# A state-attention and soft-MoE kernel: smaller matmul tiles for the folded routing weights and for the output, and combine weights turned by one VectorE transpose

## The chip, the cores and the metric

The kernel runs on one core of one Trainium2 chip. The metric is the device time of one execution, in microseconds (us); lower is better. Five engines work side by side, each through its own instructions in order: TensorE (PE in the rows; its weight loads are listed as PEld), VectorE (DVE), ScalarE (ACT), GpSimd (POOL) and SyncE (SP), whose queue here issues every DMA.

## The reference, cut to what matters

```python
# attention: x (8,8,512,64), state (8,8,32,64)
a     = softmax(0.125 * x @ state.T)            # over the 32 states
xread = a @ state
a2    = softmax(0.125 * state @ x.T)            # over the 512 tokens
sread = a2 @ x
x = concat([xread, sread], tokens)              # 4352 tokens of 512 values
# feed-forward
g = silu(x @ w_in)                              # w_in (512, 2048), given in fp64
x = g @ w_out                                   # w_out (2048, 512), given in fp64
# soft MoE, 8 experts of 4 slots: 32 slots
logits     = x @ phi                            # phi (512, 32)
d          = softmax(logits, over all tokens)
slot_input = d.T @ x                            # (32, 512)
slot_out   = per expert: relu(slot_input @ w1[e]) @ w2[e]
c          = softmax(logits, over the 32 slots)
out        = c @ slot_out                       # (4352, 512)
```

## The kernel before, in words

All operations are first recorded by a helper class, then put in an order by a list scheduler with fixed costs of its own, and issued in that order, so each engine's order of work is fixed when the program is built. Because every operation is recorded by one helper, nearly all rows of the profile carry line 333; they are told apart by the names of their tiles. A `together` block makes one unit of several TensorE calls. A tile with a tag takes its place in a ring of buffers of that tag; PSUM has the rings `h` (2 banks), `lg` (1), `w` (1) and `w2` (4), and tiles of a ring are handed out in the order in which the program names them.

**Start.** The fp64 weights are loaded as pairs of 32-bit words, half of a quarter at a time (8 pieces `raw` of w_out, then 8 of w_in), and turned into fp32 by `conv`: one ScalarE operation and five VectorE operations on 128x1024 elements. `wo_half` (line 481) does this for w_out, writes the result `win` to a DRAM scratch (`wo_f`), turns it with TensorE transposes (`wT`), and after each second half multiplies it by phi: `w2ps` holds w_out @ phi for a quarter of the 2048 hidden units, and VectorE copies it to `w2p` (lines 505 to 513). The w_out-phi product folds the second matrix of the feed-forward and phi into one 2048x32 matrix, so that logits come straight from g. Between these steps stands the attention of the first batch (`a_scores`, `a_split`, `a_soft1` to `a_soft3`, `a_eT`, `a_sread`, whose result `srs` VectorE scales out of the PSUM tile `sr`) and the first part of the second's. `win_half` then converts w_in.

**Middle.** For each of 9 blocks of tokens (`k`; 512 tokens, the last 256) `hid` makes the hidden units (`h`, 16 pieces), ScalarE and VectorE make `g` of them, VectorE transposes `g` by 32x32 blocks into `blk`, `logits` multiplies by `w2p`, `s_sum` and `s_rep` add up the partial sums (`lr`) and make the exponentials (`dT` for the slots, `cw` for the tokens), and `s_dTg` multiplies `dT` by `blk` into the four banks `S`, which are added into `acc`.

**End.** `slot_T` turns `acc` and `slot_mm` multiplies it by w_out: once for the first 8 blocks (`siaT`, `sia`), once for the last (`sibT`, `sib`); then the experts' first matrices (`f`, to `hs`, transposed as `hT`), the combine weights (lines 1060 to 1079: each block of `cw` is split by VectorE and GpSimd into two fp32r parts, turned by TensorE as `cTp` and copied by ScalarE to `cT`), and, for each half `ch` of the 512 output columns, the experts' second matrices (`so`, `sor`) and the output matmuls `o`, evicted by VectorE and ScalarE in turn and written by SP. w1 and w2 (32 pieces of 1 MB, `in_w_dram`) are loaded by `load_w` into places that other tiles have left; pieces 17 to 20 go where `wo`, the operand of `sib`, has stood.

Of the kernel before, what the change touches and what calls it, by code (L numbers as in the profile page):

```python
# [7 lines left out]
F32 = mybir.dt.float32  # L8
F32R = mybir.dt.float32r
# [357 lines left out]
def tile_state_attention_soft_moe(  # L367
# [113 lines left out]
    def wo_half(fq, half):  # L481
        n = 2 * fq + half
        if half == 0:

            wn_t[fq] = win_t[fq]
            wT_t[fq] = unit(("wb", "wb", "A", "A")[fq], [4, 4, 4, 32], f"wT{fq}")
        wn = wn_t[fq][:, 2 * half:2 * half + 2]
        conv(n, wn)
        if n >= 4:
            next_raw()  # L490
        nc.sync.dma_start(out=wo_f32[fq, :, 2 * half:2 * half + 2], in_=wn)
        for x in range(2):
            q = 2 * half + x
            p = bank("h", f"wT{fq}_{q}")
            with nc.together():
                for dc in range(4):
                    nc.tensor.transpose(p[:, dc * 128:dc * 128 + 128], wn[:, x, dc * 128:dc * 128 + 128], ident)
            nc.scalar.copy(
                out=wT_t[fq][:, :, :, q, :], in_=p.rearrange("p (d i c) -> p d i c", d=4, i=4)
            )  # L500
        if half == 0:
            return

        wT = wT_t[fq]
        p = bank("w", f"w2ps{fq}")
        with nc.together():
            for i in range(4):
                for dc in range(4):
                    mm(
                        p[:, 32 * i:32 * i + 32], lhsT=wT[:, dc, i].rearrange("p q c -> p (q c)"),  # L510
                        rhs=phi_sb[:, dc, :], start=(dc == 0), stop=(dc == 3),
                    )
        nc.vector.tensor_copy(out=w2p[:, fq].rearrange("p i s -> p (i s)"), in_=p[:, 0:128])

    def win_half(fq, half):
        n = 8 + 2 * fq + half
# [65 lines left out]
    def a_soft3(b):  # L582
        s = at[b, "s"]
        t = s[:, 1].rearrange("p h t -> p (h t)")
        nc.vector.transpose(out=t, in_=s[:, 0].rearrange("p h t -> p (h t)"))
        at[b, "ar"] = a = unit("A", [2, 2, 512], f"ar{b}", F32R)
        nc.scalar.copy(out=a[:, 0], in_=s[:, 1])
        nc.gpsimd.tensor_tensor(out=a[:, 1], in0=s[:, 1], in1=a[:, 0].bitcast(F32), op=ALU.subtract)

    def a_eT(b, h2):  # L590
        e = at[b, "e"]
# [158 lines left out]
        nc.scalar.copy(out=ls[:, :n], in_=lg_t.pop(k)[:, :n])  # L750
        sx[k, "ls"] = ls

    def tok_major(src, nt, tag, name):

        t = rot.tile([128, 4, NSLOT], F32, tag=tag, name=name, bufs=2 if tag == "ld" else 1)
        for x in range(4):
            rows = slice(32 * x, 32 * x + 32)
            nc.vector.transpose(
                out=t[rows, :nt, :],
                in_=src[rows, :nt * 128].rearrange("p (y x r) -> p x y r", x=4, r=32)[:, x],  # L760
            )
        return t[:, :nt, :]

    def s_rep(k):
# [1 line left out]
        nt = n // 128  # L766
        ls = sx.pop((k, "ls"))
        lr = bank("w", f"lr{k}")
        mm(lr[:, :n], lhsT=r44, rhs=ls[:, :n], start=True, stop=True)
        m = rot.tile([128, 4], F32, tag="m", name=f"m{k}")  # L770
        nc.vector.reduce_max(out=m[:, 0:1], in_=lr[:, :n], axis=AX.X)
        prev = m_old[0]
# [12 lines left out]
        m_old[0] = m  # L785
        sx[k, "m"], sx[k, "first"] = m, first
        if k in BY_PE:
            dT = tok_major(d, nt, "ld", f"dT{k}")
        else:
            dT = rot.tile([128, 512], F32, tag="ld", name=f"dT{k}")  # L790
            nc.vector.transpose(out=dT[:, :n], in_=d[:, :n])
# [86 lines left out]

    def slot_T(x, name):

        p = bank("w", f"{name}T")
        with nc.together():
            for q in range(4):
                for f in range(4):
                    n = 32 * (4 * q + f)
                    mm(p[:, n:n + 32], lhsT=x[:, q, f * 128:(f + 1) * 128], rhs=r4, start=True, stop=True)
        xT = rot.tile([128, 16, NSLOT], F32, tag="g", name=f"{name}Ts", bufs=NG)
        nc.vector.tensor_copy(out=xT.rearrange("p i s -> p (i s)"), in_=p)
        return xT

    def slot_mm(xT, name):
        p = bank("w", name)
        with nc.together():
            for q in range(4):
                for fq in range(4):
                    mm(
                        p[32 * fq:32 * fq + 32, :],
                        lhsT=xT[:, 4 * q + fq, :],
                        rhs=wo_t[fq][:, q, :],
                        start=(q == 0),  # L900
                        stop=(q == 3),
                    )
        return p


# [128 lines left out]
    for w in range(2):  # L1034
        hp = [bank("h", f"f1_{w}_{x}") for x in range(2)] if w == 0 else pair("f1_1")
        for dc in range(4):
            for x in range(2):
                with nc.together():
                    for e in range(4):
# [4 lines left out]
                            start=(dc == 0),  # L1044
                            stop=(dc == 3),
                        )
        load_w(28 if w == 0 else 32)
        for x in range(2):
            hs = rot.tile([128, 512], F32, tag="th", name=f"hs{w}_{x}")
            nc.scalar.activation(out=hs, in_=hp[x], func=AF.Relu, scale=masks[:, w:w + 1])  # L1050
# [6 lines left out]
            nc.vector.tensor_copy(out=hTs[:, w, x].rearrange("p i s -> p (i s)"), in_=p)  # L1057


    cT = []  # L1060
    for q in range(NB + 1):
        nt = ntok(q) // 128
        if q == NB:
            ctu = rot.tile([128, 1, 512], F32R, tag="g", name="cT8", bufs=NG)
        elif q % 4 == 0:
            ctu = unit("wb", [4, 512], f"cT{q}", F32R)
        cv = cw[:, 4 * q:4 * q + nt, :].rearrange("p t (o s) -> p t o s", o=1).to_broadcast([128, nt, 2, NSLOT])
        c2 = rot.tile([128, 4, 2, 2, NSLOT], F32, tag="th", name=f"c2_{q}")
        hi = c2[:, :nt, :, 0, :]
        nc.vector.tensor_copy(out=hi.bitcast(F32R), in_=cv)  # L1070
        nc.gpsimd.tensor_tensor(out=c2[:, :nt, :, 1, :], in0=cv, in1=hi, op=ALU.subtract)
        p = bank("w", f"cTp{q}")
        with nc.together():
            for t in range(nt):
                nc.tensor.transpose(
                    p[:, t * 128:(t + 1) * 128], c2[:, t].rearrange("p a b s -> p (a b s)"), ident
                )
        nc.scalar.copy(out=ctu[:, q % 4, :nt * 128], in_=p[:, :nt * 128])
        cT.append(ctu[:, q % 4, :])


    outb = out.rearrange("(b r) f -> b r f", r=TOK)
    n_out = 0
    obuf = [12, 14, 16, 17, 18, 19, 20, 0, 1, 2]
    for ch in range(2):
        so = bank(("lg", "h")[ch], f"so{ch}")
        with nc.together():
            for w in range(2):
                for kk in range(8):
                    for e in range(4):  # L1090
                        mm(
                            so[32 * e:32 * e + 32, 0:256],
                            lhsT=hTs[:, w, kk // 4, kk % 4, 32 * e:32 * e + 32],
                            rhs=wt["w2", 8 * ch + 4 * w + e][kk // 2][:, 256 * (kk % 2):256 * (kk % 2) + 256],
                            start=(w == 0 and kk == 0),
                            stop=(w == 1 and kk == 7),
                        )
        sos = rot.tile([128, 256], F32, tag="ld", name=f"sos{ch}")
        nc.scalar.copy(out=sos, in_=so[:, 0:256])
        p = bank(("lg", "h")[ch], f"sor{ch}")  # L1100
        mm(p[:, 0:256], lhsT=r44, rhs=sos, start=True, stop=True)
        sor = rot.tile([128, 256], F32R, tag="th", name=f"sor{ch}")
        nc.scalar.copy(out=sor, in_=p[:, 0:256])
        nc.vector.tensor_tensor(
            out=sor[64:128, :], in0=p[64:128, 0:256], in1=sor[64:128, :].bitcast(F32), op=ALU.subtract
        )
        cols = slice(256 * ch, 256 * ch + 256)
        for q in range(NB + 1):
            nt = ntok(q) // 128
            if q % 2 == 0:  # L1110
                obu = place(obuf[5 * ch + q // 2]).rearrange("p (a t f) -> p a t f", a=2, t=4)
            ob = obu[:, q % 2]
            for t in range(0, nt, 2):
                tag = ("w", "w2", "w2", "h", "w2", "w2", "h")[n_out % 7]
                p = bank(tag, f"o{n_out}")
                with nc.together():
                    for x in range(2):
                        mm(
                            p[:, 256 * x:256 * x + 256], lhsT=cT[q][:, (t + x) * 128:(t + x + 1) * 128], rhs=sor,
                            start=True, stop=True,  # L1120
                        )
                (nc.scalar.copy if n_out % 2 else nc.vector.tensor_copy)(
                    out=ob[:, t:t + 2, :].rearrange("p t f -> p (t f)"), in_=p
                )
                n_out += 1
            if q < NB:
                nc.sync.dma_start(
                    out=outb[q, 0:512, cols].rearrange("(t p) f -> p t f", p=128), in_=ob
                )
            else:  # L1130
                for t in range(nt):
                    nc.sync.dma_start(out=outb[4 * t:4 * t + 4, 512:TOK, cols], in_=ob[:, t, :])
    for k in range(NB + 1):

        for op in exps.get(k + 1, []):
# [50 lines left out]
```

## Time and profile before

| | us |
|---|---|
| median of 3 runs (lowest, highest) | 582.49 (582.3, 584.6) |
| profiled execution | 581.93 |
| its span, first to last instruction | 580.1 |
| TensorE busy | 485.5 |
| VectorE busy | 355.6 |
| ScalarE busy | 274.6 |
| GpSimd busy | 102.9 |

The profiled execution takes 1.83 us more than its span. Shares of busy time are averages over stages that differ; the stage has to be read before a share means anything. The clock of TensorE is given as a share of full speed (1.00 is 2.4 GHz, 0.50 is 1.2 GHz).

### The profile page before, as it was taken

The numbers are of one execution on the slowest core, as the hardware profiler recorded it, in microseconds if no ns is written. First come the engines' busy times: TensorE is split into PE (matmuls) and PEld (weight loads), VectorE is DVE, ScalarE is ACT, GpSimd is POOL, SyncE is SP. The second block draws the span as 40 slices with busy tenths as digits, with TensorE's granted clock in tenths as the row PEclk, the third lists the DMA queues.
The fourth block names the chain that finished last, engine by engine and source line by source line (L and its number), as shares of the span: only waits on it lengthen the run. The fifth ranks groups of instructions, "written<-read, shape, count | busy, mean of one in ns | idle before, by whom it ended". The sixth has DMA issues, their size and how long they took to land.

```text
span 580.1 us, 10381 instructions
## 1 busy us (share of the span) xinstructions
PE 485.5 (84%) x4380; PEld 299.6 (52%) x4380; DVE 355.6 (61%) x610; ACT 274.6 (47%) x471; POOL 102.9 (18%) x65
## 2 busy tenths in 40 slices
PE   2456672897999989989989999999999997897760
PEld 1446671564646546546555555465557792434640
DVE  5776568997396676686785785784763934111430
ACT  3522331864764754754845845745735523011430
POOL 0000010001213232232232222223006330003100
PEclk9985555898999999999999999999999998799795
DMA  8975554420202202202202202103033299599796
GB/s 340 410 271 181 188 182 141 150 73 0 73 2 73 74 1 73 73 3 73 72 2 74 73 2 79 68 1 147 1 138 154 95 424 363 218 424 421 283 295 199
DMA packets 21566, 85.79 MB, mean 148 GB/s; under 512 B 1552, under 2 KB 10640, under 8 KB 13840
## 3 DMA queue, kind: packets, MB, share of 16 engines
q1 hardware_dynamic: 21520, 85.14, 39.5%
q8 instruction: 34, 0.56, 0.4%
q14 instruction: 12, 0.10, 0.0%
HBM read 72.03 MB, written 13.11 MB: 147 GB/s over the span
## 4 chain that ended last, share of the span: by engine, by line
PE 69%; DVE 17%; ACT 7%; issue 3%; POOL 1%; DMA 1%; DVEq 0%; ACTq 0%; POOLq 0%
PE h L333 31%; PE S L333 7%; DVE win L333 5%; PE w2ps L333 5%; PE wbp L333 5%; PE lg L333 4%; DVE acc L333 3%; PE f L333 2%; PE so L333 2%; PE sr L333 2%; PE wT L333 1%; ACT e L333 1%; ACT wb L333 1%; DVE lt L333 1%; DVE wb L333 1%
## 5 line engine op out<-in xcount | busy, mean ns | idle before, releaser
L333 PE MATMUL h<-ar,wb 128*128 128x512 f32 x768 | 198.9, 407 | 3.8 <-DVE wb L333 2.1
L333 PEld LDWEIGHTS h<-ar,wb 128*128 128x128 f32 x768 | 140.2, 190 | 66.1 <-issue 13.9
L333 ACT ACTIVATE g<-h 128x512 f32<-128x512 f32 (+1 forms) x108 | 62.0, 575 | 109.3 <-PE h L333 107.5
L333 DVE STREAM_TRANSPOSE blk<-g 128x512 f32<-128x512 f32 (+1 forms) x128 | 83.5, 666 | 38.2 <-ACT g L333 37.8
L333 POOL TENSOR_TENSOR wb<-wf,wb 128x512 fp32r<-128x512 f32 x28 | 36.0, 1286 | 126.3 <-ACT wf L333 81.5
L333 POOL TENSOR_TENSOR ar<-s,ar 128x1024 fp32r<-128x1024 f32 x8 | 19.1, 2388 | 179.8 <-ACT ar L333 179.8
L333 PE MATMUL wbp<-win,ss 64*32 64x512 f32 x512 | 36.4, 626 | 13.0 <-DVE win L333 13.0
L333 ACT CAST wb<-wbp 128x512 fp32r<-128x512 f32 x64 | 34.6, 595 | 26.7 <-PE wbp L333 26.7
L333 PE MATMUL lg<-g,w2p 128*32 128x512 f32 (+1 forms) x288 | 43.8, 581 | 0.0
L333 PE MATMUL S<-blk,dT 32*32 32x512 f32 (+1 forms) x992 | 38.9, 611 | 3.4 <-DVE dT L333 2.8
L333 DVE TENSOR_TENSOR wb<-wbp,wb 128x512 fp32r<-128x512 f32 x36 | 24.4, 687 | 23.6 <-ACT wb L333 23.4
L333 PE MATMUL wT<-cst,win 128*128 128x128 f32 x64 | 15.6, 424 | 24.0 <-DVE win L333 15.9
L333 POOL TENSOR_TENSOR s<-s,tm 128x1024 f32<-128x1024 f32 x12 | 23.3, 1938 | 52.3 <-DVE tm L333 37.1
L333 ACT ACTIVATE th<-h 128x512 f32<-128x512 f32 (+1 forms) x36 | 20.6, 571 | 21.9 <-PE h L333 21.9
L333 PE MATMUL w2ps<-phi,wT 128*128 128x32 f32 x128 | 28.1, 402 | 2.7 <-ACT wT L333 2.7
L333 PEld LDWEIGHTS w2ps<-phi,wT 128*128 128x128 f32 x128 | 27.6, 332 | 4.3 <-ACT wT L333 4.3
L333 PEld LDWEIGHTS wT<-cst,win 128*128 128x128 f32 x64 | 12.7, 226 | 28.8 <-issue 17.1
L333 ACT ACT_TABLE_LOAD x21 | 26.9, 1283 | 1.1 <-PEq L1176 0.7
L333 DVE TENSOR_REDUCE tm<-s 128x32 f32<-128x1024 f32 x16 | 19.4, 1214 | 13.1 <-ACT s L333 13.1
L333 ACT COPY wT<-wT 128x512 f32<-128x512 f32 x16 | 9.4, 586 | 37.6 <-PE wT L333 37.6
L333 DVE SCALAR_TENSOR_TENSOR acc<-acc,m,S 128x512 f32<-128x512 f32 x28 | 19.1, 741 | 12.2 <-PE S L333 12.2
L333 DVE SCALAR_TENSOR_TENSOR g<-th,h 128x512 f32<-128x512 f32 (+1 forms) x36 | 23.0, 646 | 4.2 <-ACT th L333 4.0
(118 smaller groups left out, 688.1 us busy)
## 6 DMA issues: line engine op xcount, KB each, us to landing
place<-in_w_dram SPq DMA_DIRECT2D x17, 1024.0 KB, 12.1
blk<-in_w_dram SPq DMA_DIRECT2D x15, 1024.0 KB, 9.4
raw<-in_w_out_dram SPq DMA_DIRECT2D x8, 1024.0 KB, 14.4
xT<-in_xT_dram SPq DMA_DIRECT2D x8, 1024.0 KB, 4.7
xk<-in_xk_dram SPq DMA_DIRECT2D x8, 1024.0 KB, 5.5
raw<-in_w_in_dram SPq DMA_DIRECT2D x8, 1024.0 KB, 4.8
out_dram<-place SPq DMA_DIRECT2D x10, 512.0 KB, 6.5
wo_f<-win SPq DMA_DIRECT2D x8, 512.0 KB, 5.8
```

The source lines that it names most:

```text
L333: made = [call(*args, **kwargs) for call, args, kwargs in op.calls]
```

## The change

Seven edits, and nothing else in the program:

1. `w2ps`: instead of 16 calls with a 128x128 piece of `wT` as weights and 32 columns of phi moving, 4 calls with phi as 128x32 weights and 512 columns of `wT` moving, in the four column tiles of one bank; ScalarE copies the bank (`w2s`, `s2`), 4 calls add up the four parts and turn them (`w2q`), and ScalarE, no longer VectorE, makes the copy to `w2p`.
2. The subtraction that makes `ar` of the first batch moves from GpSimd to VectorE.
3. `tok_major` orders the tokens of `lt` by x, y, r where it was y, x, r; `dT` of block 0 keeps the old order.
4. `slot_T` takes its bank from `w2`, `slot_mm` from `h`, where both took `w`; `sia` is made to come after `lr` of the last block.
5. Some of the calls of `load_w` stand earlier, inside the loop over `f`.
6. The combine weights: the loop over 9 blocks is replaced by one VectorE transpose of `cw` by 32x32 blocks.
7. The output: `so` is issued as 16 groups of 4 calls, not one of 64; `sor` is one fp32 copy by VectorE; `o` is made by fp32 32x32 tiles with 256 columns, two blocks of tokens into four banks at a time, and the DMAs of the two blocks follow when the four banks are copied. The last block has 4 output DMAs per half instead of 2.

```diff
-            for i in range(4):
-                for dc in range(4):
-                    mm(
-                        p[:, 32 * i:32 * i + 32], lhsT=wT[:, dc, i].rearrange("p q c -> p (q c)"),
-                        rhs=phi_sb[:, dc, :], start=(dc == 0), stop=(dc == 3),
-                    )
-        nc.vector.tensor_copy(out=w2p[:, fq].rearrange("p i s -> p (i s)"), in_=p[:, 0:128])
+            for dc in range(4):
+                mm(
+                    p[32 * dc:32 * dc + 32, :], lhsT=phi_sb[:, dc, :],
+                    rhs=wT[:, dc].rearrange("p i q c -> p (i q c)"), start=True, stop=True,
+                )
+        s2 = rot.tile([128, 512], F32, tag="ld", name=f"w2s{fq}")
+        nc.scalar.copy(out=s2, in_=p)
+        p = bank("w", f"w2q{fq}")
+        with nc.together():
+            for i in range(4):
+                mm(p[:, 32 * i:32 * i + 32], lhsT=s2[:, i * 128:(i + 1) * 128], rhs=r4, start=True, stop=True)
+        nc.scalar.copy(out=w2p[:, fq].rearrange("p i s -> p (i s)"), in_=p[:, 0:128])
...
-        nc.gpsimd.tensor_tensor(out=a[:, 1], in0=s[:, 1], in1=a[:, 0].bitcast(F32), op=ALU.subtract)
+        (nc.gpsimd if b else nc.vector).tensor_tensor(out=a[:, 1], in0=s[:, 1], in1=a[:, 0].bitcast(F32), op=ALU.subtract)
...
-        p = bank("w", f"{name}T")
+        p = bank("w2", f"{name}T")
...
-        p = bank("w", name)
+        p = bank("h", name)
...
+        if name == "sia":
+            nc.after(first, sx[NB, "lr"])
...
+            if dc == 1:
+                load_w(25 if w == 0 else 31)
+            if dc == 3:
+                load_w(28 if w == 0 else 32)
...
+    cT = unit("wb", [2048], "cT")[:, 0:34 * NSLOT]
+    nc.vector.transpose(out=cT, in_=cw.rearrange("p t s -> p (t s)"))
...
-        so = bank(("lg", "h")[ch], f"so{ch}")
-        with nc.together():
-            for w in range(2):
-                for kk in range(8):
+        so = bank("lg", f"so{ch}")
+        for w in range(2):
+            for kk in range(8):
+                with nc.together():
...
+            tags = ("w2", "w2", "w2", "w2") if q // 2 % 2 == 0 else ("h", "h", "w", "lg")
+            p = [bank(t, f"o{ch}_{q}_{x}") for x, t in enumerate(tags)]
...
+                for a in both:
+                    for y in range(nt):
+                        for x in range(4):
+                            n = NSLOT * (4 * (q + a) + y)
+                            mm(
+                                p[x][32 * y:32 * y + 32, 256 * a:256 * a + 256],
+                                lhsT=cT[32 * x:32 * x + 32, n:n + 32],
+                                rhs=sor[32 * x:32 * x + 32, :],
+                                start=True,
+                                stop=True,
+                            )
```

## Rows read from the trace of the kernel before

**Rows 1.** Waits of VectorE, first 140 us: total us, times, longest.

```profile
DVE w2p L333 <- PE w2ps L333: 19.1, 4, 6.0
DVE win L333 <- ACT win L333: 6.8, 1, 6.8
DVE srs L333 <- PE sr L333: 3.9, 1, 3.9
```

**Rows 2.** Timeline of the start: start, us, engine, operation [idle before <- releaser].

```profile
66.44 0.29 DVE L333 COPY w2p<-w2ps 128x128 f32<-128x128 f32 x1 [5.98 <-PE w2ps L333]
66.65 1.21 DVE L333 TENSOR_TENSOR win<-win,acc 128x1024 f32<-128x1024 f32 x1
...
71.75 1.22 DVE L333 TENSOR_TENSOR win<-win,acc 128x1024 f32<-128x1024 f32 x1
...
75.09 0.59 ACT L333 COPY wT<-wT 128x512 f32<-128x512 f32 x1 [0.27 <-PE wT L333]
...
75.73 7.04 PE L333 MATMUL w2ps<-phi,wT 128*128 128x32 f32 x32 [0.68 <-ACT wT L333]
...
76.72 3.42 DVE L333 SCALAR_TENSOR_TENSOR acc<-raw,acc 128x1024 f32<-128x1024 uint32 x1
...
82.80 0.29 DVE L333 COPY w2p<-w2ps 128x128 f32<-128x128 f32 x1 [2.66 <-PE w2ps L333]
...
83.15 1.11 PE L333 MATMUL eT<-cst,e 128*128 128x128 f32 x4 [0.39 <-DVE w2p L333]
...
88.73 0.48 DVE L333 TENSOR_SCALAR srs<-sr,asm 128x64 f32<-128x64 f32 x2 [3.91 <-PE sr L333]
```

**Rows 3.** Timeline: one 16-record group early and late, and a logits group.

```profile
98.87 1.96 PE L333 MATMUL wbp<-win,ss 64*32 64x512 f32 x16 [9.06 <-DVE win L333]
...
111.15 1.09 PE L333 MATMUL wbp<-win,ss 64*32 64x512 f32 x16 [1.17 <-DVE win L333]
...
112.76 1.06 PE L333 MATMUL lg<-g,w2p 128*32 128x512 f32 x8
```

**Rows 4.** Chain that ended last, whole span (start, us, what): the middle.

```profile
211.48 1.07 PE S L333 x32
...
253.94 1.07 PE S L333 x32
```

**Rows 5.** The same chain from 476 us on.

```profile
481.35 0.71 PE lr L333 x2
...
484.03 1.95 PE S L333 x32
485.98 4.41 PE sia L333 x32
...
516.55 4.43 PE f L333 x40
...
531.70 0.60 PE cTp L333 x4
...
542.87 5.12 PE o L333 x30
...
548.66 7.16 PE so L333 x128
```

**Rows 6.** Windows: stretch, us, engines busy, granted clock, DMA share, GB/s.

```profile
540.00:543.00 3.00, 1.88 (x7) 1.15 (x7) 0.43 (x1) 1.17 (x4) 0.45 (x1) 0.50 0.69 287
543.00:546.00 3.00, 3.00 (x15) 3.00 (x16) 1.83 (x3) 1.59 (x4) 0.00 (x0) 0.55 0.08 28
555.00:560.00 5.00, 3.53 (x35) 2.56 (x28) 1.71 (x4) 2.26 (x6) 0.00 (x0) 1.00 0.78 236
...
575.00:580.00 5.00, 0.00 (x0) 0.00 (x0) 0.00 (x0) 0.00 (x0) 0.00 (x0) 0.50 0.27 84
```

**Rows 7.** Window during the loads: TensorE busy, granted clock, DMA share, GB/s.

```profile
510.00:515.00 5.00, 5.00 (x52) 1.00 1.01 423
```

**Rows 8.** Group: copies out of PSUM at the output; busy us, mean ns.

```profile
L333 DVE COPY place<-o 128x512 f32<-128x512 f32 x11 | 7.0, 683 | 2.2 <-PE o L333 2.2
```

More of the change, by code (lines that the diff above doesn't have):

```diff
@@ L751, in s_sum, with tok_major @@
         sx[k, "ls"] = ls
-    def tok_major(src, nt, tag, name):
+    def tok_major(src, nt, tag, name, order="x y r"):
         t = rot.tile([128, 4, NSLOT], F32, tag=tag, name=name, bufs=2 if tag == "ld" else 1)
@@ L759, in tok_major @@
                 out=t[rows, :nt, :],
-                in_=src[rows, :nt * 128].rearrange("p (y x r) -> p x y r", x=4, r=32)[:, x],
+                in_=src[rows, :nt * 128].rearrange(f"p ({order}) -> p x y r", x=4, r=32)[:, x],
             )
@@ L768, in s_rep @@
         lr = bank("w", f"lr{k}")
-        mm(lr[:, :n], lhsT=r44, rhs=ls[:, :n], start=True, stop=True)
+        sx[k, "lr"] = mm(lr[:, :n], lhsT=r44, rhs=ls[:, :n], start=True, stop=True)
         m = rot.tile([128, 4], F32, tag="m", name=f"m{k}")
@@ L891, in slot_mm @@
     def slot_mm(xT, name):
-        p = bank("w", name)
+        p = bank("h", name)
+        first = None
         with nc.together():
@@ L895, in slot_mm @@
                 for fq in range(4):
[L896 removed]
+                    op = mm(
                         p[32 * fq:32 * fq + 32, :],
@@ L902, in slot_mm @@
                     )
+                    first = first or op
+        if name == "sia":
+            nc.after(first, sx[NB, "lr"])
         return p
@@ L1057, in tile_state_attention_soft_moe @@
             nc.vector.tensor_copy(out=hTs[:, w, x].rearrange("p i s -> p (i s)"), in_=p)
[L1060 to L1072, printed above, removed]
-        with nc.together():
[L1074 to L1079, printed above, removed]
+    cT = unit("wb", [2048], "cT")[:, 0:34 * NSLOT]
+    nc.vector.transpose(out=cT, in_=cw.rearrange("p t s -> p (t s)"))
     outb = out.rearrange("(b r) f -> b r f", r=TOK)
-    n_out = 0
     obuf = [12, 14, 16, 17, 18, 19, 20, 0, 1, 2]
     for ch in range(2):
-        so = bank(("lg", "h")[ch], f"so{ch}")
-        with nc.together():
-            for w in range(2):
-                for kk in range(8):
+        so = bank("lg", f"so{ch}")
+        for w in range(2):
+            for kk in range(8):
+                with nc.together():
                     for e in range(4):
@@ L1099, in tile_state_attention_soft_moe @@
         nc.scalar.copy(out=sos, in_=so[:, 0:256])
-        p = bank(("lg", "h")[ch], f"sor{ch}")
+        p = bank("lg", f"sor{ch}")
         mm(p[:, 0:256], lhsT=r44, rhs=sos, start=True, stop=True)
[L1102 to L1106, printed above, removed]
+        sor = rot.tile([128, 256], F32, tag="th", name=f"sor{ch}")
@@ L1107, in tile_state_attention_soft_moe @@
+        nc.vector.tensor_copy(out=sor, in_=p[:, 0:256])
         cols = slice(256 * ch, 256 * ch + 256)
-        for q in range(NB + 1):
+        for q in range(0, NB + 1, 2):
+            ob = place(obuf[5 * ch + q // 2]).rearrange("p (x a f) -> p x a f", x=4, a=2)
+            tags = ("w2", "w2", "w2", "w2") if q // 2 % 2 == 0 else ("h", "h", "w", "lg")
+            p = [bank(t, f"o{ch}_{q}_{x}") for x, t in enumerate(tags)]
             nt = ntok(q) // 128
[L1110 to L1123, printed above, removed]
@@ new lines, in tile_state_attention_soft_moe @@
+            both = range(2) if q < NB else range(1)
+            with nc.together():
+                for a in both:
[9 more added lines that the diff above has]
+                            )
@@ L1124, in tile_state_attention_soft_moe @@
+            for x in range(4):
+                r = slice(0, 32 * nt)
+                (nc.scalar.copy if x % 2 else nc.vector.tensor_copy)(
+                    out=ob[r, x, 0:len(both)].rearrange("p a f -> p (a f)"), in_=p[x][r, 0:256 * len(both)]
                 )
-                n_out += 1
             if q < NB:
-                nc.sync.dma_start(
-                    out=outb[q, 0:512, cols].rearrange("(t p) f -> p t f", p=128), in_=ob
-                )
-            else:
-                for t in range(nt):
-                    nc.sync.dma_start(out=outb[4 * t:4 * t + 4, 512:TOK, cols], in_=ob[:, t, :])
+                for a in both:
+                    nc.sync.dma_start(
+                        out=outb[q + a, 0:512, cols].rearrange("(t p) f -> p t f", p=128), in_=ob[:, :, a]
+                    )
+            else:
+                for x in range(4):
+                    nc.sync.dma_start(out=outb[2 * x:2 * x + 2, 512:TOK, cols], in_=ob[0:64, x, 0])
```

3 lines of the change are left out of this document (1 added, 2 removed).

## Prediction

> **What bounds the kernel now.** I read the waits of each engine first, then the timeline of the first 140 us, then the chain of work that ended last, and at the end the windows with the DMA share. Three stages with three limits come out.
>
> In the start the limit is VectorE. In its first 140 us it waits for four things only, and three of them stand in [rows 1]: 6.8 us for the first converted word, 19.1 us in four copies of `w2p`, each standing behind `w2ps` on TensorE, and 3.9 us before `srs`. What the reader is to see in [rows 2] is that the copy, a 0.29 us instruction, sits in front of the conversions on an in-order engine: VectorE stood 5.98 us before the copy at 66.44 us, and the conversion's last addition follows it 0.21 us later.
>
> In the middle the limit is TensorE. The chain of waits is matmul after matmul, and the `S` group comes back at 211.48 and 253.94 us, 42.46 us apart [rows 4]. No edit touches a matmul of that period, so I carry it over unchanged: what the start saves arrives at the end in full.
>
> In the end it is first TensorE, then DMA. While the experts' matrices are loaded the DMA share is 1.01 at 423 GB/s [rows 7]. Then it falls to 0.69 and to 0.08 between 540 and 546 us, and to 0.78 between 555 and 560 [rows 6]: the loads are through, and the first output isn't ready, because the transposes `cTp` run from 531.70 up to the first `o` at 542.87 [rows 5]. In 575 to 580 us the share is 0.27: the last writes drain.
>
> **The change part by part.**
>
> *Edit 1, the first three quarters.* The long waits of three copies go with the copies themselves, which ScalarE now makes. All four waits sum to 19.1 us and the fourth is 2.66 [rows 1, 2], so three are 16.4; three copies' steps of 0.21 add 0.6. Sum 17.1 us. What VectorE does next (the addition, then the next piece) needs only words that ScalarE has prepared: after the first, VectorE never waited for `win` from ScalarE [rows 1].
>
> *Edit 1, the last quarter.* Here VectorE next stands before `srs`, which hangs on TensorE: `w2ps`, `eT`, `sr`. Old path from the start of `w2ps` to the start of `eT`: 83.15 - 75.73 = 7.42 us [rows 2]. New path: 8 records of 512 columns in column tiles, which `lg` makes in 1.06 us [rows 3]. That is at the later speed; in the start the 16 records of `wbp` took 1.96 us, later 1.09 [rows 3], so 1.06 x 1.8 = 1.9. Then a copy of 128x512 out of PSUM, 0.59 [rows 2]; 8 records of the old kind, 7.04 / 32 = 0.22 each, 1.76; a copy of 128x128, 0.3 (VectorE's took 0.29); four hand-overs of about 0.07. Sum 4.8, gain 2.6 us. Bounds: nothing (should the two extra hand-overs be slow), and the whole of what VectorE loses in this piece besides, if it finds other work to do ahead of `srs`: 2.6 + 3.9, and 1.0 for edit 2 (next), 7.5. I take 2.6, because the order of instructions around `srs` comes from the same list scheduler and the wait of 3.91 stands there already.
>
> *Edit 2.* VectorE's operation at 76.72 takes 3.42 us where its neighbours of the same kind (the rows' 1.21 us addition is the nearest) take little over a third: GpSimd's subtraction runs beside it. The change takes away some 2.2 and puts one two-input operation of 1.2 on VectorE, 1.0 net. It lies inside the wait for `srs`, so I cost it at nothing; if that cover is gone it is worth the 1.0 counted in the bound above.
>
> *Edit 3* keeps number and shape of the transposes; the nearest row for a price is none better than themselves: 0. If reading the tokens in a row were slower or faster by half, it would be hidden under TensorE in every block but the last.
>
> *Edit 4.* Now TensorE ends `lr` at 482.06, stands until 484.03, makes the first half of `S`, then `sia`, then the second half [rows 5]. With a bank of its own `sia` fills the gap: 1.97 us. After the gap the first `S` half takes 1.95 us for 32 records where 1.07 is the usual [rows 4, 5], and `sia` 4.41 for 32 where 40 of `f` took 4.43, so 3.54 at that pace. Without a gap these 0.88 and 0.87 should go too. Sum 3.7 us; bounds 2.0 (the gap alone) and 3.7. I take 3.7: nothing else idles TensorE there. Loads 17 to 20 wait for the end of `sib`, so the stream of loads starts as much earlier.
>
> *Edit 5.* A load can start only when the `f` group before it has freed its place, whatever line it stands on, and at 510 us the DMA engines are already full [rows 7]. Cost 0, no gain either.
>
> *Edit 6* removes all of `cTp` and what ScalarE and VectorE do for it. The new transpose is one VectorE operation of 1088 columns, at most twice the 0.683 of a 512-column copy [rows 8], while TensorE makes `f`. From 531.70 to 542.87 are 11.2 us, of which making `sor` (one matmul like `lr`, 0.71, and two copies of 256 columns) needs about 2. TensorE could thus start `o` some 9 us earlier. But DMA then is the limit: what can be gained is the time in which it stands: 0.31 x 3 + 0.92 x 3 + 0.22 x 5 = 4.8 us [rows 6]. I take 4.8; bounds 0, and 4.8 plus the drain, 0.73 x 5 = 3.65.
>
> *Edit 7.* The output matmuls: 136 calls of 32x32 tiles per half, 272 records. 32 records of 512 columns take 1.07 us when 16 tiles work together [rows 4]; for 256 columns between half and all of that, so 4.5 to 9.1 us per half, against 5.8 from the first `o` to `so` now (542.87 to 548.66 [rows 5]). Four banks are copied by two engines, two 0.683 copies each, so the first output DMA of a half comes about 1.1 + 1.4 = 2.5 us after its first `o`. Is it hidden? Half 0: `so` ends at 531.7 - 3.7 = 528.0, `o` starts at about 530, the DMAs are queued from 532.5. The loads end near 542 - 3.7 = 538. The writes of half 0, 4.46 MB at 236 / 0.78 = 303 GB/s, then take until 552.7. Half 1 needs the last load, half of `so` (3.6 us), `sor` (2) and 2.5: 546. So there are over 6 us of cover, which also pay for four more DMAs and for the later issue of pairs of blocks. If the cover is gone, each us late is a us lost.
>
> The Trainium skill (TensorEngine Tiling, Key Properties) says that a change of tiling mode drains TensorE. Edit 7 lets groups of `so` (128x32) stand between groups of `o` (32x32), so this speaks against it. The nearest row is `lg`, which stands among 128x128 work and takes 1.06 where 8 records at the pace of `f` take 0.89: some 0.17 a change, and ten changes, two for each of five output groups, are 1.7 us, inside the cover. By the rule with nothing overlapped it would be more, which no row here prices.
>
> **Sum.** Start 17.1 + 2.6 = 19.7. End 3.7 + 4.8 = 8.5. Span 580.1 - 28.2 = 551.9; plus the 1.83 us around the span, 553.7. The median of the runs shown lies 0.56 above the profiled execution: 554.
>
> **Rivals.**
>
> *The end gives only edit 4 (0.15).* The output stage is late by its cover: banks shared by `so` and `o`, changes of tile size, pairs of blocks before a DMA. For it: one bank `lg` serves both halves of `so` and an output bank. Against: 6 us. Time 554 + 4.8 = 559; if even edit 4 is lost, 562.
>
> *The wait moves from TensorE to ScalarE (0.12).* ScalarE is in order too. If its preparing operation for the next but one piece stands behind the new copies, VectorE waits. From the end of a second half's conversion (71.75 + 1.22) to the start of `w2ps` are 2.8 us [rows 2], to the new `w2p` copy 4.8 more, and about 1.2 to prepare 1024 columns (two copies of 512 at 0.59), against 5.1 for the piece between (66.65 to 71.75): 3.7 us in each of three quarters, 11.1. Time 565. Against: no such wait now [rows 1].
>
> *More than that (0.06).* VectorE also loses the wait for `srs`, and the drain shortens: 554 - 4.9 - 3.65 = 545.5.
>
> *Slower: tiles of one column group take turns (0.04).* In `S` successive calls go along column tiles, in the new `o` along row tiles, which no row shows. One record of 512 columns alone takes 0.44 (four in 0.44 in `f`), of 256 0.22; one at a time, 272 are 60 us a half, 120 in all, where now about 17 + 6 are spent: 554 + 97 - 4.8 is over 640. It decides when a half takes more than about 23 us, that is with fewer than 2.6 tiles at work together. Against: 16 work together in `S` [rows 4].
>
> *No change (0.03).* The start's waits reappear in full elsewhere: a DMA-bound start. Against: after the first piece no row of [rows 1] names a DMA.
>
> **Chances and range.** The forecast has 0.60. Its own range takes the bounds: start 17.1 to 24.6, end 2.0 to 12.2: 545.7 to 563.4. The range over the cases, with the ScalarE rival in and the slow one out, is 544 to 566. A difference under 0.5% can't be told from none: faster 0.93, same 0.03, slower 0.04.
>
> **What would show it.** Right: no wait of VectorE for `w2ps`, and `srs` near 69 us, not 88.73; a wait for `srs` of 3 to 5 us; the period of `S` still 42.5; `lr`, `sia`, `S` without a gap, `sia` at 3.5; DMA full from the loads to the last writes. Wrong: VectorE waiting for `win` from ScalarE in the start; a longer period in the middle, since the scheduler orders the whole program anew; `o` slower than 9 us a half; DMA idle between loads and writes.

## The result and the profile after

| kernel | median of its runs, us | range | runs |
|---|---|---|---|
| before, on the same chip | 582.86 | 582.3 to 584.6 | 4 |
| after | 557.49 | 554.34 to 560.75 | 4 |

The ratio is 0.956, with an interval of 0.950 to 0.962: 25.4 us less, where 28.2 were forecast. The profiled execution took 560.75 us (span 559.0), the longest of its four. A later run of the same kernel (called the repeat below) has a span of 555.7; why one kernel has two spans comes with the clock, further down.

First the waits of VectorE in the first 122 us of the kernel after (engine, what waited <- what it waited for: us in total, times, longest):

```profile
DVE win L333 <- ACT win L333: 6.7, 1, 6.7
DVE srs L333 <- PE sr L333: 2.6, 1, 2.6
DVE ar L333 <- ACT ar L333: 1.6, 1, 1.6
...
DVE asm L333 <- ACT e L333: 0.6, 1, 0.6
```

The line of 19.1 us for `w2p` in [rows 1] is gone. The single wait for the first word is still there and no second one has joined it. The wait for `srs` is shorter than the old 3.9. Two small waits are new: the subtraction that edit 2 put on VectorE stands 1.6 us behind ScalarE's part of it, and a sum (`asm`) stands 0.6 us behind ScalarE's exponentials.

The timeline of the start of the kernel after, the last quarter of `w_out` (start, us, engine, operation [idle before <- releaser]), against [rows 2]:

```profile
59.48 1.93 PE L333 MATMUL w2ps<-wT,phi 128*32 128x512 f32 x8 [0.91 <-ACT wT L333]
60.40 1.23 DVE L333 TENSOR_TENSOR ar<-s,ar 128x1024 fp32r<-128x1024 f32 x1 [1.55 <-ACT ar L333]
61.48 0.59 ACT L333 COPY w2s<-w2ps 128x512 f32<-128x512 f32 x1 [1.11 <-PE w2ps L333]
62.11 1.92 PE L333 MATMUL w2q<-cst,w2s 128*128 128x32 f32 x8 [0.70 <-ACT w2s L333]
64.07 0.27 ACT L333 COPY w2p<-w2q 128x128 f32<-128x128 f32 x1 [0.49 <-PE w2q L333]
64.39 1.12 PE L333 MATMUL eT<-cst,e 128*128 128x128 f32 x4 [0.36 <-ACT w2p L333]
69.97 0.47 DVE L333 TENSOR_SCALAR srs<-sr,asm 128x64 f32<-128x64 f32 x2 [2.61 <-PE sr L333]
```

From `w2ps` to `eT` are 64.39 - 59.48 = 4.91 us (old path 7.42, forecast 4.8), and `srs` comes at 69.97 instead of 88.73.

The chain that ended last, kernel after (start, us, what), against [rows 4] and [rows 5]:

```profile
191.13 1.07 PE S L333 x32
...
233.60 1.07 PE S L333 x32
...
463.99 0.70 PE lr L333 x2
464.69 3.57 PE sia L333 x32
468.26 2.18 PE S L333 x57
...
511.83 1.54 PE o L333 x62
...
516.84 2.48 issue
...
521.87 9.75 PE so L333 x128
...
533.29 2.81 PE o L333 x114
```

The first of these `S` groups comes 20.35 us earlier than before, and the next 42.47 us after it, where it was 42.46: the start gave 20.35 and the middle took nothing. (Each trace is one execution. In the other kernels with this start, which come below, the same group stands between 190.6 and 193.6 us, so a us or two of the 20.35 change from one execution to the next.) `lr` and `sia` now follow each other without a gap. No `cTp` stands in the chain any more, and `o` starts at 511.83 where it was 542.87.

The windows at the end of the kernel after (stretch, us, each engine's busy time, granted clock, DMA share, GB/s), against [rows 6]:

```profile
511.00:514.00 3.00, 2.48 (x116) 1.76 (x125) 1.05 (x3) 0.60 (x2) 0.00 (x0) 1.00 1.01 421
...
535.00:540.00 5.00, 4.89 (x202) 2.68 (x177) 4.10 (x7) 3.48 (x7) 0.00 (x0) 1.00 0.69 213
540.00:545.00 5.00, 0.02 (x2) 0.00 (x0) 1.46 (x4) 1.15 (x4) 0.00 (x0) 0.92 1.02 345
...
550.00:555.00 5.00, 0.00 (x0) 0.00 (x0) 0.00 (x0) 0.00 (x0) 0.00 (x0) 0.50 0.20 65
555.00:559.00 4.00, 0.00 (x0) 0.00 (x0) 0.00 (x0) 0.00 (x0) 0.00 (x0) 0.50 0.09 29
```

The gap between loads and writes is closed: `o` begins while the loads still run at a share of 1.01. But from 550 on the core does nothing except move data, at a share of 0.20 and then 0.09. Before, only the last window was as low, at 0.27 [rows 6]. The same is seen in the milestones, taken from the timelines and chains:

| us from the start of the span | before | after | the repeat | with another write of the last block (e6) |
|---|---|---|---|---|
| `siaT` starts | 469.5 | 449.1 | 449.2 | 449.7 |
| `sib` ends | 503.2 | 484.0 | 479.5 | 481.7 |
| last `f` ends | 521.0 | 501.8 | 497.2 | 499.5 |
| last `o` ends | 562.4 | 540.0 | 535.4 | 537.8 |
| span ends | 580.1 | 559.0 | 555.7 | 550.2 |
| last `o` to the end | 17.7 | 19.0 | 20.3 | 12.4 |

The last `o` of the repeat is 27 us earlier than before, its end only 24.4: the end of the kernel gave something back after TensorE had finished.

### The profile page after: what moved, and what is told of

Same layout as the page of the kernel before. It is cut to its first block, busy times and chain, and to the rows that moved or that the text cites. A ratio compares the mean times of both kernels' runs of the same rounds, so it can differ in the third digit from the quotient of the medians.

```text
span 559.0 us, 11107 instructions
## 1 busy us (share of the span) xinstructions
PE 475.4 (85%) x4758; PEld 279.2 (50%) x4758; DVE 353.8 (63%) x602; ACT 272.9 (49%) x471; POOL 94.3 (17%) x55
## 4 chain that ended last, share of the span: by engine, by line
PE 68%; DVE 15%; ACT 8%; issue 4%; POOL 1%; DMA 1%; DVEq 0%; ACTq 0%; POOLq 0%
PE h L333 34%; PE S L333 7%; DVE win L333 4%; PE lg L333 4%; PE wbp L333 4%; DVE acc L333 3%; PE so L333 3%; PE f L333 3%; PE o L333 2%; PE sr L333 2%; ACT e L333 2%; ACT wb L333 1%; DVE lt L333 1%; PE eT L333 1%; PE sib L333 1%
## 5 line engine op out<-in xcount | busy, mean ns | idle before, releaser
L333 POOL TENSOR_TENSOR ar<-s,ar 128x1024 fp32r<-128x1024 f32 x7 | 16.8, 2398 | 162.3 <-ACT ar L333 162.3
L333 DVE TENSOR_TENSOR wb<-wbp,wb 128x512 fp32r<-128x512 f32 x36 | 24.4, 687 | 24.1 <-ACT wb L333 23.9
L333 DVE SCALAR_TENSOR_TENSOR acc<-acc,m,S 128x512 f32<-128x512 f32 x28 | 19.1, 743 | 12.2 <-PE S L333 12.2
L333 PE MATMUL h<-s,w8h 128*128 128x256 f32 x128 | 26.7, 307 | 0.0
L333 PEld LDWEIGHTS h<-s,w8h 128*128 128x128 f32 x128 | 21.7, 206 | 4.5 <-issue 1.4
L333 PEld LDWEIGHTS wbp<-win,ss 64*32 64x32 f32 x512 | 5.9, 105 | 34.9 <-issue 13.9
L333 ACT ACTIVATE win<-raw 128x1024 f32<-128x1024 f32 x16 | 18.5, 1163 | 9.7 <-DMA raw<-in_w_out_dram 5.4
## 6 DMA issues: line engine op xcount, KB each, us to landing
place<-in_w_dram SPq DMA_DIRECT2D x17, 1024.0 KB, 12.4
```

The lines of the kernel that those rows point to most:

```text
L333: made = [call(*args, **kwargs) for call, args, kwargs in op.calls]
```

## The experiments

Each was run in five rounds beside the kernel before; us are medians (range), the ratio is to the kernel before on that chip, and the span is that of the profiled execution.

| run | kernel | us | ratio (interval) | span |
|---|---|---|---|---|
| e1 | before + edits 1, 2 | 567.04 (562.88 to 568.39) | 0.9705 (0.9669 to 0.9742) | 565.4 |
| e2 | before + edits 3 to 7 | 576.86 (574.86 to 577.77) | 0.9891 (0.9859 to 0.9922) | 572.8 |
| e3 | before, copy of `w2p` on ScalarE | 567.04 (565.23 to 570.21) | 0.9728 (0.9693 to 0.9762) | 567.1 |
| e4 | before + tiles of edit 1, last copy on VectorE | 570.93 (567.79 to 573.75) | 0.9784 (0.9746 to 0.9822) | 568.3 |
| e5 | after, again (the repeat) | 558.16 (555.86 to 559.05) | 0.9561 (0.9536 to 0.9586) | 555.7 |
| e6 | after, last block's writes by rows | 551.03 (548.84 to 552.44) | 0.9439 (0.9411 to 0.9466) | 550.2 |
| e7 | after, output in 32x128 tiles | 557.11 (555.39 to 559.59) | 0.9550 (0.9520 to 0.9580) | 557.7 |
| e8 | e6 and e7 together | 552.20 (546.97 to 553.01) | 0.9442 (0.9405 to 0.9478) | 550.4 |
| e9 | e6 + one load earlier | 549.56 (546.62 to 550.36) | 0.9406 (0.9374 to 0.9439) | 547.7 |
| e10 | before + edit 4 | 580.93 (579.36 to 582.52) | 0.9959 (0.9935 to 0.9982) | 579.4 |
| e11 | after without edit 2 | 555.92 (555.51 to 560.22) | 0.9538 (0.9499 to 0.9577) | 554.5 |
| e12 | after without edit 5 | 557.54 (556.12 to 559.76) | 0.9557 (0.9525 to 0.9589) | 558.0 |

**The two halves of the change: e1 and e2.** e1 is the kernel before with the hunks of edits 1 and 2 alone (two of their lines):

```diff
+        nc.scalar.copy(out=w2p[:, fq].rearrange("p i s -> p (i s)"), in_=p[:, 0:128])
...
+        (nc.gpsimd if b else nc.vector).tensor_tensor(out=a[:, 1], in0=s[:, 1], in1=a[:, 0].bitcast(F32), op=ALU.subtract)
```

e2 is the kernel before with all the others (again two lines):

```diff
+        p = bank("h", name)
...
+    cT = unit("wb", [2048], "cT")[:, 0:34 * NSLOT]
```

> The kernel before with edits 1 and 2 alone (w_out times phi by column tiles with ScalarE's copies, and the first batch's ar subtraction on VectorE); the whole result is computed. Theory: the start is bound by VectorE, and the middle carries what it saves to the end in full, so the time falls by the 19.7 us of the sum (20.4 by the trace of the changed kernel at the first S group), to about 563. Rival: the end takes part of it back (loads or writes that can't start earlier), and the time falls by 15 or less, to 568 or more.

> The kernel before with edits 3 to 7 alone (sia ahead of S, one transpose for the combine weights, output by 32x32 tiles, loads placed earlier); the whole result is computed. By the forecast's sum the time falls by 8.5 us, to about 574. Rival, from the profile of the changed kernel, whose last writes drain for 7 us at some 45 GB/s: the end gives only 1 to 5 us, 578 to 582.

The ratios make 17.2 us for the start alone (15.0 to 19.3) and 6.4 for the end alone (4.5 to 8.2); together 23.6, where the whole change gives 25.6 in the repeat. So the parts roughly add up, and both are under their forecasts, 19.7 and 8.5; each time lies between what its forecast and its rival gave. In e1 the first `S` group of the list above stands at 191.01, 20.5 us earlier than before, as in the kernel after: the start saved its full forecast, and some 3 us of that didn't reach the end of e1. Its trace shows where part of it went. `siaT` still starts 20.5 us earlier than before, the first `o` only 14.9 (527.99 instead of 542.87). Between the two the first 72 records of `f` take 9.63 us, and 7.93 before, and the first `so` takes 8.73 us, and 7.04 before; the granted clock is 0.76 from 505 to 510 in e1, and 1.00 in all of that `so` before.

**Who carries the start: e3 and e4.** e3 moves nothing but the copy:

```diff
-        nc.vector.tensor_copy(out=w2p[:, fq].rearrange("p i s -> p (i s)"), in_=p[:, 0:128])
+        nc.scalar.copy(out=w2p[:, fq].rearrange("p i s -> p (i s)"), in_=p[:, 0:128])
```

e4 is the kernel before with the column tiles of edit 1, and leaves the last copy where it was (some of its lines; the last one is unchanged):

```diff
+                    p[32 * dc:32 * dc + 32, :], lhsT=phi_sb[:, dc, :],
...
+        s2 = rot.tile([128, 512], F32, tag="ld", name=f"w2s{fq}")
+        nc.scalar.copy(out=s2, in_=p)
...
+                mm(p[:, 32 * i:32 * i + 32], lhsT=s2[:, i * 128:(i + 1) * 128], rhs=r4, start=True, stop=True)
         nc.vector.tensor_copy(out=w2p[:, fq].rearrange("p i s -> p (i s)"), in_=p[:, 0:128])
```

> The kernel before with one word changed: the copy from w2ps to w2p is made by ScalarE, not by VectorE; the 16 calls of w2ps stay as they were. Theory: the copy's place on the in-order VectorE is the whole cost in the first three quarters, so 16 to 18 us go although TensorE works as long as before: about 565. Rival: TensorE's 7 us per quarter are what counts, and the time stays at 582, or ScalarE now stands in VectorE's place and delays the words that VectorE needs: 571 or more.

> The kernel before with the column tiles of edit 1, but with the last copy (w2q to w2p) on VectorE as before. Theory: VectorE again stands before each copy, for about 4.8 us from the start of w2ps instead of 7.1, so only some 2 to 3 us of each of the four waits go: 8 to 11 us in all, about 573. Rival: the shorter TensorE work is what helps, and nearly all of e1's gain is there: about 563.

The waits of VectorE in the first 122 us of e3:

```profile
DVE srs L333 <- PE sr L333: 8.3, 1, 8.3
DVE win L333 <- ACT win L333: 6.8, 1, 6.8
```

and of e4:

```profile
DVE win L333 <- ACT win L333: 6.9, 1, 6.9
DVE w2p L333 <- PE w2q L333: 6.7, 4, 2.3
DVE srs L333 <- PE sr L333: 3.9, 1, 3.9
```

In e3 the waits for `w2p` have left VectorE, but one comes back: `srs` now takes 8.3 us instead of 3.9, since the slow `w2ps` still stands ahead of it on TensorE. By the first `S` group (196.50) e3 has gained 15.0 of the 20.35. In e4 the path is short but VectorE still stands behind it four times, 6.7 us; its `S` comes at 199.09, a gain of 12.4, the whole fall of that wait (19.1 to 6.7), and more than the 8 to 11 us expected. Each alone gives more than half, and the two overlap: 15.0 + 12.4 is over 20.35. So most of the start can be had either way, by letting another engine wait or by making the wait shorter. What the column tiles add to e3 at this point is 5.4 us (with edit 2, which e11 below puts at nothing); the wait for `srs` is 5.7 shorter with them (8.3 to 2.6). In the times this doesn't show: e1 and e3 have the same median, 567.04, and their intervals overlap. That the column tiles gain time beyond the moved copy is seen in the traces of the start, and not shown at the end.

**Edit 4 alone: e10.**

```diff
-        p = bank("w", f"{name}T")
+        p = bank("w2", f"{name}T")
...
-        p = bank("w", name)
+        p = bank("h", name)
...
+        if name == "sia":
+            nc.after(first, sx[NB, "lr"])
```

> The kernel before with edit 4 alone (sia and its bank, and the bank of the turns); the whole result is computed. The forecast's term: 3.7 us less at the start of the loads after sib, and as that stream sets the end, 3.7 us at the end: about 579. By the runs with edits 3 to 7, where sib ended 5.2 us earlier: up to 5. Rival: the clock falls later instead, under sibT and sib, and only the 2 us of the gap go: about 581.

The chain of e10:

```profile
482.79 0.70 PE lr L333 x2
483.49 3.57 PE sia L333 x32
487.06 2.18 PE S L333 x57
490.17 3.74 PE sibT L333 x32
...
526.69 9.47 PE so L333 x128
...
542.38 5.12 PE o L333 x30
```

and two lines of the chain before, beside those in [rows 5]:

```profile
492.19 4.99 PE sibT L333 x32
...
524.65 7.04 PE so L333 x128
```

The gap is gone, `sia` runs at 3.57 (forecast 3.54) and all of `S` at its usual pace. From `lr` to the start of `sibT` are 490.17 - 482.79 = 7.38 us, where the kernel before takes 10.84, from its `lr` at 481.35 [rows 5] to its `sibT` at 492.19: 3.5 us less, close to the forecast 3.7. The experts' `f` starts 3.6 us earlier (502.02 instead of 505.59). What the rival named doesn't appear: `sibT` takes 3.74 us, less than before. At the end 2.4 us are left (1.0 to 3.8), an interval that holds the forecast 3.7 and the rival's 2 alike. In this one execution the chain shows where TensorE lost again what it had gained: its first `so` takes 9.47 us, and 7.04 before, and the first `o` comes at 542.38, 0.5 us earlier than before. The granted clock is 0.57 from 523 to 533 in e10, and 1.00 from 524 to 532 before. The loads are not what held it up: they are through by 540 (DMA share 0.41 from 538 to 540), where before the share is 0.95 as late as 540 to 542.

**Edits 2 and 5 taken back: e11 and e12.**

```diff
-        (nc.gpsimd if b else nc.vector).tensor_tensor(out=a[:, 1], in0=s[:, 1], in1=a[:, 0].bitcast(F32), op=ALU.subtract)
+        nc.gpsimd.tensor_tensor(out=a[:, 1], in0=s[:, 1], in1=a[:, 0].bitcast(F32), op=ALU.subtract)
```

```diff
-            if dc == 1:
-                load_w(25 if w == 0 else 31)
-            if dc == 3:
-                load_w(28 if w == 0 else 32)
+        load_w(28 if w == 0 else 32)
```

> The changed kernel with edit 2 taken back (the first batch's ar subtraction on GpSimd again); the whole result is computed. The forecast costs the edit at nothing, hidden in the wait for srs: the time stays at 557.5 within 1.5 us, and the wait for srs, 2.6 us in the changed kernel, differs by what VectorE no longer does or loses. Rival: GpSimd's run slows VectorE's conversion where nothing hides it, and 2 us or more come back.

> The changed kernel with edit 5 taken back (the loads recorded after the loop over f again); the whole result is computed. The forecast: nothing, since a load starts when its place is free, whatever line it stands on; within 1.5 us of 557.5. Rival: the loads start later and the stream with them, 2 us or more.

Both intervals hold the repeat's 0.9561: neither edit can be told from nothing, to within some 2 us. The cover named for edit 2 is there. The wait of VectorE in e11 is the same as in the kernel after, though VectorE's addition takes 3.26 us where it takes 1.22 in the kernel after; GpSimd's subtraction runs beside it, from 60.80 to 63.31 us:

```profile
DVE srs L333 <- PE sr L333: 2.6, 1, 2.6
```

```profile
61.13 3.26 DVE L333 TENSOR_TENSOR win<-win,acc 128x1024 f32<-128x1024 f32 x1
```

**The drain: e5, e6.** The kernel after writes the last block, 64 KB at a time, in DMAs whose outermost dimension is 2. e6 writes the same bytes with 32 rows outermost, two DMAs for each half instead of four:

```diff
-                for x in range(4):
-                    nc.sync.dma_start(out=outb[2 * x:2 * x + 2, 512:TOK, cols], in_=ob[0:64, x, 0])
+                for y in range(nt):
+                    nc.sync.dma_start(
+                        out=outb[:, 512:TOK, cols].rearrange("(x y) r f -> y r x f", y=2)[y],
+                        in_=ob[32 * y:32 * y + 32, :, 0],
+                    )
```

> The changed kernel once more, as the measure for the next three. By its first four runs: 557.5 us, 554 to 561. Its writes should drain at the end as before, with a DMA share near 0.13 for some 7 us.

> The changed kernel, with the last block's writes split otherwise: 2 DMAs per half whose outermost dimension is the 32 rows, where the change has 4 whose outermost dimension is the 2 batches; the same bytes in the same 1 KB pieces, the whole result computed. Theory: a share of 0.13 is 2 of 16 engines, so each of the change's small writes lies on two engines and the four follow each other there; spread over all, the 7 us at 45 GB/s go and the time falls by 4 to 6 us, to about 552.5. Rival: the 7 us are the time that the last write needs to land, whatever its shape, and the time stays within 1 us of the changed kernel's.

The last windows of the repeat (stretch, us, TensorE busy, granted clock, DMA share, GB/s):

```profile
547.00:549.00 2.00, 0.00 (x0) 0.50 0.15 43
549.00:551.00 2.00, 0.00 (x0) 0.50 0.11 28
551.00:553.00 2.00, 0.00 (x0) 0.50 0.13 48
```

and of e6:

```profile
546.00:548.00 2.00, 0.00 (x0) 0.50 1.04 308
548.00:550.00 2.00, 0.00 (x0) 0.50 0.21 47
```

A share of 0.13 of 16 engines is two engines: the outermost dimension of the four writes. With 32 rows outermost the share stays full until 548 and the low stretch of some 7 us is 2. The time falls from 558.16 to 551.03, 7.1 us, with intervals that are far apart, and more than the 4 to 6 us expected. e6 also has two DMAs a half instead of four; that the width counts and not the number is read from the share, which stays near two engines for the whole 7 us, and was not tried apart. The Trainium skill (DMA: Bandwidth & Descriptors, "Why a DMA increments its semaphore by 16 and not by 1") says that a DMA is spread over the largest number of engines, up to 16, that divides the slowest dimension other than 1 of both its sides, so 2 for the one form and 16 for the other. The two traces agree with it: 0.13 for the one, and for the other a share of 1.04 up to 548 with no long stretch at a low share behind it.

**Fewer output matmuls: e7 and e8.** e7 joins four 32x32 tiles to one of 32x128, a quarter of the calls:

```diff
-                    for y in range(nt):
-                        for x in range(4):
-                            n = NSLOT * (4 * (q + a) + y)
-                            mm(
-                                p[x][32 * y:32 * y + 32, 256 * a:256 * a + 256],
-                                lhsT=cT[32 * x:32 * x + 32, n:n + 32],
...
+                    for x in range(4):
+                        n = NSLOT * 4 * (q + a)
+                        mm(
+                            p[x][0:32 * nt, 256 * a:256 * a + 256],
+                            lhsT=cT[32 * x:32 * x + 32, n:n + 32 * nt],
```

> The changed kernel, with the output made by tiles of 32 rows and 128 columns: one call where the change has four, 34 per half and not 136, the same columns streamed, the whole result computed. Theory: the change's 1088 records of output matmuls and weight loads make TensorE wait for its instructions (2.5 us at 516.8, behind full DMA engines), and that gap lets the clock fall to 0.50 under the second so (9.8 us, not 7.2); with a quarter of the calls both go, and since DMA stands for some 1.6 us meanwhile, the time falls by 1 to 4 us, to about 555. Rival 1: DMA is the bound all through, and nothing changes. Rival 2: four tiles of 128 columns work less side by side than sixteen of 32, and the time rises by 2 to 6 us.

> The changed kernel with both of these edits, the whole result computed. If both theories hold and their gains add up: 5 to 9 us less than the changed kernel, 549 to 552. If the output is bound by DMA and only the drain counts: the same as with the writes alone, about 552.5.

Five lines of e7's timeline:

```profile
508.00 2.01 PE L333 MATMUL o<-sor,cT 32*128 32x256 f32 x32 [0.52 <-DVE sor L333]
...
510.65 2.34 PE L333 MATMUL o<-sor,cT 32*128 32x256 f32 x32 [0.65 <-DVE place L333]
513.23 0.66 PE L333 MATMUL o<-sor,cT 32*64 32x256 f32 x8 [0.23 <-DVE blk L333]
514.15 3.66 PE L333 MATMUL so<-blk,place 128*32 128x256 f32 x64 [0.27 <-ACT place L333]
...
521.57 0.40 PE L333 MATMUL so<-blk,place 128*32 128x256 f32 x1 [2.27 <-DMA blk<-in_w_dram]
```

The 2.48 us of "issue" in the chain of the kernel after are gone: the groups of `o` wait for copies alone. The second `so` starts at the higher clock, 64 records in 3.66 us; the granted clock stays at 1.00 from 505 to 535, where in the kernel after it is 0.53 from 520 to 525, right behind the gap. So both the gap and the fall of the clock go, as the theory said. The time isn't lower all the same (0.9550 against 0.9561, e8 0.9442 against e6's 0.9439), as the first rival said: in this stretch the loads set the end, and TensorE waits for them instead, 2.27 us for one of them.

**One load earlier: e9.** The kernel of e6, with one 1 MB piece of the experts' matrices loaded into `acc` as soon as `sibT` has read it, ahead of `sib` (the main lines; the numbers of the later pieces and places move with it):

```diff
-    p = slot_mm(slot_T(acc, "sib"), "sib")
+    sibT = slot_T(acc, "sib")
+    load_w(18)
+    p = slot_mm(sibT, "sib")
```

> The changed kernel with the last block's writes spread over all DMA engines, and one of the 32 pieces of w1 and w2 loaded into acc as soon as the turn of its last contents is done, so that it needn't wait for sib; the whole result is computed. Theory: from the loads after sib to the end the kernel is bound by DMA, and a piece of 1 MB taken out of that stream into the 6 us before, when DMA stands, saves its own 2.5 us: about 548.5. Rival: the chain of so, sor and o sets the end, and the time stays at the 551 of the writes alone.

The 4 us about the end of `sib` in e9, where `sib` ends at 479.5 (stretch, us, TensorE busy, granted clock, DMA share, GB/s):

```profile
476.00:480.00 4.00, 3.47 (x28) 0.85 0.68 272
```

and in e6, where it ends at 481.8:

```profile
478.00:482.00 4.00, 3.73 (x28) 0.78 0.04 18
```

The idle stretch of DMA ahead of the experts fills as meant: (0.68 - 0.04) x 4 = 2.6 us of transfers are now done there. The time is the lowest of all, 549.56 us; its ratio lies 0.0033 under that of e6, some 1.9 us, but the intervals overlap: e9 is not shown to be faster than e6. Both beat the kernel before and the kernel after.

## Why the prediction was right, point by point

- **The sum, 28.2 forecast, 25.4 measured.** The start gave a little more than its term and the end 5.0 of its 8.5 (25.4 less 20.35). In the end two errors pull against each other, as the point on edits 6 and 7 shows: a cost that was left out, some 7 us, and a gain that was sized too small. That the whole comes so near is in part luck.
- **Start, 19.7 forecast, 20.35 measured** at the first `S` group. The rival in which ScalarE takes over the wait fell: no second wait for `win` appears. The three quarters were not measured by themselves: e3, which moves all four copies and nothing else, gives 15.0 and not 17.1, because `srs` waits 4.4 us longer then. The column tiles, for which the forecast counts 2.6 in the last quarter, are worth 5.4 at this point beside the moved copies. The wait for `srs`, foreseen at 3 to 5 us, is 2.6.
- **Middle, nothing forecast:** 42.47 against 42.46 us a period.
- **Edit 4, 3.7 forecast:** 3.5 on TensorE in e10, 2.4 at its end. Right in mechanism on TensorE and for the start of the loads. That it reaches the end in full isn't shown: the interval (1.0 to 3.8) allows it, and the one trace loses most of it again in a slower `so`, for which the prediction has no term.
- **Edits 2 and 5 at nothing:** e11 and e12 show no difference. Edit 3 was not run alone.
- **Edits 6 and 7, 4.8 forecast.** The step that failed is the sentence that over 6 us of cover "also pay for four more DMAs and for the later issue of pairs of blocks". I counted the four DMAs by their number. What they cost was their width: two engines of 16, some 7 us after everything else was done. e6 gives 7.1 us back. "DMA full from the loads to the last writes", named as a sign of being right, didn't come. Nor was the cover 6 us: DMA still stands for 0.31 x 5 = 1.6 us between the writes of the two halves (the window at 535), and in e6 for 1.4 (a share of 0.83 from 530 to 538). The end alone gives 6.4 us (e2) where 8.5 were forecast. With the writes of e6 the whole gain is 32.7 us (0.0561 x 583.55), so that some 12 are the end's: about its upper bound of 3.7 + 4.8 + 3.65, the drain gone.
- **The output matmuls, 4.5 to 9.1 us a half:** half 1 took 6.73 us for 272 records. The slower rival, tiles that take turns, fell with that.
- **The end gives only edit 4, 559 us:** this rival has the right place, an end that gives less, and the median of 557.5 is nearer to its 559 than to 554, so that the time alone doesn't decide against it. Its mechanism is small, though. In the chain of the kernel after, waits for copies out of the banks take 1.4 us between the groups of `o` in half 0 (513.38 to 514.81) and 1.1 ahead of the second `so` (520.76 to 521.87), while the loads still hold DMA at a share of 1.01; in half 1 all 272 records follow each other.
- **A drain at each change of tile size** was put inside the cover. TensorE's order put all of the first half's `o` ahead of the second `so`, so that the alternation hardly occurs; no run here shows what a change costs.

The forecast of 554 lies just below the fastest of the four runs (554.3 to 560.8). The prediction also has no term for TensorE's clock (below). That explains some of the spread of the runs, but not the distance to the median: the profiled execution of the repeat, without the fall of the clock shown below, took 557.45 us.

## What to carry to other kernels

A short instruction that waits for a slow partner costs most on the engine that has other work behind it: look first at which engine stands in the queue, and then at how to make the partner faster. Price a DMA by the shape of its outermost dimension as well as by its bytes, above all the last ones of a kernel, which nothing covers. Time saved on TensorE while the loads bound the kernel turns into a wait for the loads: e7 lost a gap of 2.48 us, got a wait of 2.27 and was no faster.

## What was not expected of the hardware

**Three lengths of the same stretch.** From `siaT` to `lr` the same work took 11.9 us in some of the profiled executions (before, e2, e4, e5, e7, e11), 13.4 in others (e1, e3, e9, e10) and 14.9 in four (after, e6, e8, e12). A window in it, kernel after (stretch, us, TensorE busy with its records, granted clock, DMA share, GB/s):

```profile
452.00:454.00 2.00, 2.00 (x11) 0.52 1.02 430
454.00:456.00 2.00, 2.00 (x11) 0.50 1.02 430
```

and the repeat, the same kernel:

```profile
452.00:454.00 2.00, 2.00 (x19) 1.00 1.02 430
454.00:456.00 2.00, 2.00 (x22) 1.00 1.01 422
```

TensorE is busy throughout in both. In one the granted clock is at its lower level, 1.2 GHz, with half the records in 2 us; in the other at 2.4 GHz. The engine had been busy ahead of it in both (450 to 452: 2.00 of 2.00 at 1.00). By the end of `sib` the kernel after lies 4.5 us behind the repeat (484.0 against 479.5), and 4.6 by the end of the last `o`; its shorter drain takes 1.3 back, and 3.3 are left between the two spans. What makes the clock fall in one execution and not in the other stays open.

**TensorE stood for 2.48 us with nothing to wait for.** It stands in the middle of the small output matmuls of half 0, and a gap of 2.2 to 2.7 us stands at the same place in e2, e5, e6, e9, e11 and e12 (timeline of the kernel after):

```profile
519.32 1.75 PE L333 MATMUL o<-sor,cT 32*32 32x256 f32 x58 [2.48 <-issue]
```

The DMA queues of the kernel after in the output stage have this line for loads of instructions (packets, MB, share of 16 engines):

```profile
q8 instruction: 5, 0.08, 1.1%
```

and e7 has:

```profile
q8 instruction: 2, 0.03, 0.3%
```

One of the five lies just ahead of the gap, while the loads hold all DMA engines at a share of 1.02. With a quarter of the matmul calls (e7) both the gap and three of the packets are gone. That the gap is a wait for code is what these lines suggest; it was not shown apart from the other things that e7 changes.
